# Linear attention with a gated MLP: a rewrite with two tokens to a row, 64x64 attention tiles and a written-out order

## The chip, the cores and the metric

The kernel runs on one core of one Trainium2 chip. Its time is the device time of one execution in microseconds (us). The times are medians over several runs; the profile is that of one execution.

## The reference

Inputs are q, k and v of shape (batch 4, heads 8, tokens 768, 64), a decay `lam` for each head, and the weights of a gated MLP. All are float32, as is the output (4, 768, 512).

```
# attention, token blocks of 64; Dmask[i,j] = lam^(i-j) for i >= j, else 0
intra = (q_b @ k_b.T * Dmask) @ v_b
inter = (q_b * lam^(pos+1)) @ state
out_b = intra + inter
state = lam^64 * state + (k_b * lam^(63-pos)).T @ v_b
# x = out as (4, 768, 512); then
h = relu(x @ w_in)                     # 512 -> 1024, split into u and v
v_n = (v - mean(v)) / sqrt(var(v) + 1e-6)
v_s = w_spatial @ v_n + b_spatial      # over the tokens, 768 x 768
out = (u * v_s) @ w_out                # 512 -> 512
```

The block size of the attention is free as far as the result goes: the sum over all earlier tokens with weight lam^(distance) is what is computed.

## The kernel before, in words

The work is cut into 12 steps: 4 batches, each with three steps of 256 tokens. A step is two chunks of 128 tokens.

- `load_step` (L65) issues five loads on SyncE's queue: k and v one chunk at a time (a partition holds one token of each chunk, so a row in memory is 64 floats, 256 bytes), and q with two neighbouring tokens to a partition (512 bytes). Buffers hold four steps.
- `cast_step` (L144) makes bf16: `kd`, k times a decay that is the same for every chunk (VectorE in the first three steps, GpSimd after), `qc` on ScalarE and `vc` on GpSimd.
- `trans_step` (L157) transposes `kd` and `qc` on TensorE (16 transposes, L163). ScalarE takes out `kT`; VectorE takes out `qT` times a table of decays `lq`.
- `scores_step` (L177): 16 matmuls (L189), heads in pairs on the two row halves of the array, 128 keys against 128 queries. VectorE multiplies by `amask` (L192), a causal mask with a factor for each head.
- `kv_step` (L198): the products of `kd` and `vc` (L207). The state of a chunk is the old one times lam^128 plus this product: `sd` (L218) and `s` (L219), on VectorE.
- `out_step` (L222): state times q (L242) and masked scores times v (L249) add up in PSUM; ScalarE takes `xT` out (L252).
- The MLP: `pv` (L269: 512 columns, ReLU, statistics, normalisation `vn`), `pu` (L292: the u half), `wt_piece` (L329: w_spatial transposed once), `pvs` (L301: six matmuls of 384 columns, then a seventh at L309 that adds the bias by a matrix of 1/128 against a broadcast bias; VectorE multiplies by u, L311), `po` (L316: the last product; a store of 256 rows for each step).

PSUM is four buffers of two banks, used in turn by all of these. TensorE and GpSimd run in the order of the program text: a step's scores, outputs and key-value products, with pieces of MLP work between them taken from a list (`fill`, `after_out`). On the other engines a scheduler places the instructions. All loads of q, k and v and all stores go through SyncE's queue; the weights go through GpSimd's queue, which casts them to bf16 on the way.

Of the kernel before, what the change touches and what calls it, by code (L numbers as in the profile page):

```python
# [8 lines left out]
FP32 = mybir.dt.float32  # L10
# [4 lines left out]
PE = mybir.EngineType.PE  # L15
# [3 lines left out]
def kernel(  # L19
# [13 lines left out]
    P = 128  # L33
# [4 lines left out]
    NBLK = S // P  # L38
    NG = H // 2
    NCH = DM // P  # L40
    NR = S // (2 * P)
    NS = B * NR
    T2 = 2 * P
    HW_ = S // 2

    const = ctx.enter_context(tc.tile_pool(name="const", bufs=1))
    wpool = ctx.enter_context(tc.tile_pool(name="wpool", bufs=1))
    fin = ctx.enter_context(tc.tile_pool(name="fin", bufs=4))
    att = ctx.enter_context(tc.tile_pool(name="att", bufs=3))
    gml = ctx.enter_context(tc.tile_pool(name="gml", bufs=1))  # L50
    xpool = ctx.enter_context(tc.tile_pool(name="xpool", bufs=2))
    small = ctx.enter_context(tc.tile_pool(name="small", bufs=2))
    ostg = ctx.enter_context(tc.tile_pool(name="ostg", bufs=3))
    psum = ctx.enter_context(tc.tile_pool(name="psum", bufs=4, space=bass.MemoryType.PSUM))

    def two_banks(shape, name, dt=FP32):
        return psum.tile(shape, dt, tag="ps", name=name)


    lam_bc = const.tile([P, H], FP32)  # L60
    nc.scalar.dma_start(out=lam_bc, in_=lam.unsqueeze(0).to_broadcast((P, H)))

    st = {}

    def load_step(n):  # L65
        b, r = divmod(n, NR)
        toks = slice(r * T2, (r + 1) * T2)
        q_in = fin.tile([P, H, 2, D], FP32, tag="q_in", name=f"q_in_{n}")
        k_in = fin.tile([P, H, 2, D], FP32, tag="k_in", name=f"k_in_{n}")
        v_in = fin.tile([P, H, 2, D], FP32, tag="v_in", name=f"v_in_{n}")  # L70
        for c in range(2):
            nc.sync.dma_start(out=k_in[:, :, c, :],  # L72
                              in_=k[b, :, toks][:, c * P:(c + 1) * P].rearrange("h p d -> p h d"))
        nc.sync.dma_start(out=q_in.rearrange("p h m d -> p h (m d)"),  # L74
                          in_=q[b, :, toks].rearrange("h (p m) d -> p h (m d)", m=2))
        for c in range(2):
            nc.sync.dma_start(out=v_in[:, :, c, :],  # L77
                              in_=v[b, :, toks][:, c * P:(c + 1) * P].rearrange("h p d -> p h d"))
        st[n] = {"q_in": q_in, "k_in": k_in, "v_in": v_in}

    load_step(0)
    ident = const.tile([P, P], BF16)
    make_identity(nc, ident)

    def iota_f(shape, pattern, base, mult, name):
        ti = const.tile(shape, I32, name=name + "_i")
        nc.gpsimd.iota(ti, pattern=pattern, base=base, channel_multiplier=mult)
        tf = const.tile(shape, FP32, name=name)
        nc.vector.tensor_copy(out=tf, in_=ti)
        return tf  # L90

    krev = iota_f([P, 1], [[0, 1]], P - 1, -1, "krev")

    qpos = iota_f([P, 2, 2, D], [[1, 2], [0, 2], [2, D]], 1, 0, "qpos")

    rel = iota_f([P, 2, D], [[1, 2], [2, D]], 0, -1, "rel")

    win_sb = wpool.tile([P, NCH, DFF], BF16)
    wout_sb = wpool.tile([P, NCH, DM], BF16)
    bsp_bc = wpool.tile([P, S], BF16)  # L100
    wt_sb = wpool.tile([P, NBLK, S], BF16)
    wsp_raw = wpool.tile([P, NBLK, S], BF16)

    def load_win(f0, f1):
        nc.gpsimd.dma_start(out=win_sb[:, :, f0:f1],
                            in_=moe_w_in.rearrange("(g p) f -> p g f", p=P)[:, :, f0:f1])

    load_win(DH, DFF)
    for n in range(1, 4):
        load_step(n)  # L110


    loglam = const.tile([P, H], FP32)
    nc.scalar.activation(out=loglam, in_=lam_bc, func=AF.Ln)
    logl = const.tile([P, NG], FP32)
    for hh in range(2):
        rows = slice(hh * D, (hh + 1) * D)
        nc.vector.tensor_copy(out=logl[rows, :], in_=loglam[rows, hh::2])
    ldec = const.tile([P, H], FP32)
    nc.scalar.activation(out=ldec, in_=loglam, func=AF.Exp, scale=krev[:, 0:1])  # L120
    lq = const.tile([P, NG, T2], BF16)
    for g in range(NG):
        nc.scalar.activation(out=lq[:, g, :], in_=qpos.rearrange("p m a d -> p (m a d)"),
                             func=AF.Exp, scale=logl[:, g:g + 1])
    l128 = const.tile([P, NG], FP32)
    nc.scalar.activation(out=l128, in_=logl, func=AF.Exp, scale=float(P))
    lm128 = const.tile([P, H], FP32)
    nc.scalar.activation(out=lm128, in_=loglam, func=AF.Exp, scale=-float(P))
    causal = const.tile([P, P], FP32)
    nc.vector.tensor_scalar(out=causal, in0=rel.rearrange("p m d -> p (m d)"), scalar1=0.0,  # L130
                            scalar2=None, op0=ALU.is_ge)
    amask = const.tile([P, 2, 2, 2, P], FP32)
    for h in range(H):
        nc.vector.tensor_scalar(out=amask[:, h // 4, h % 2, (h // 2) % 2, :], in0=causal,
                                scalar1=lm128[:, h:h + 1], scalar2=None, op0=ALU.mult)
    eps_t = const.tile([P, 1], FP32)
    nc.vector.memset(eps_t, 1e-6)
    oo128 = const.tile([P, P], BF16)
    nc.vector.memset(oo128, 1.0 / P)


    xT = {}

    def cast_step(n):  # L144
        s = st[n]
        kd = att.tile([P, 2, H, D], BF16, tag="kd", name=f"kd_{n}")
        qc = att.tile([P, 2, H, D], BF16, tag="qc", name=f"qc_{n}")
        vc = att.tile([P, H, 2, D], BF16, tag="vc", name=f"vc_{n}")
        eng = nc.vector if n < NR else nc.gpsimd
        eng.tensor_tensor(out=kd.rearrange("p c h d -> p h c d"), in0=s["k_in"],  # L150
                          in1=ldec.unsqueeze(2).unsqueeze(3).broadcast_to((P, H, 2, D)),
                          op=ALU.mult)
        nc.scalar.activation(out=qc.rearrange("p m h d -> p h m d"), in_=s["q_in"], func=AF.Copy)  # L153
        nc.gpsimd.tensor_copy(out=vc, in_=s["v_in"])  # L154
        s["kd"], s["qc"], s["vc"] = kd, qc, vc

    def trans_step(n):  # L157
        kd, qc = st[n]["kd"], st[n]["qc"]
        pt = two_banks([P, 2, NG, T2], f"pt_{n}", BF16)
        for j, src in ((0, kd), (1, qc)):  # L160
            for g in range(NG):
                for c in range(2):
                    nc.tensor.transpose(  # L163
                        out=pt[:, j, g, c * P:(c + 1) * P],
                        in_=src[:, c, 2 * g:2 * g + 2, :].rearrange("p h d -> p (h d)"),
                        identity=ident)
        kT = att.tile([P, NG, T2], BF16, tag="kT", name=f"kT_{n}")
        nc.scalar.activation(out=kT, in_=pt[:, 0], func=AF.Copy)  # L168
        qT = att.tile([P, NG, 2, 2, D], BF16, tag="qT", name=f"qT_{n}")
        nc.vector.tensor_tensor(out=qT.rearrange("p g m a d -> p g (m a d)"), in0=pt[:, 1],  # L170
                                in1=lq, op=ALU.mult)
        st[n]["qT"], st[n]["kT"] = qT, kT

    def qblk(n, g, hh, c):
        return st[n]["qT"][hh * D:(hh + 1) * D, g, :, c, :]

    def scores_step(n):  # L177


        kT = st[n]["kT"]  # L180
        a_sb = att.tile([P, 2, 2, 2, 2, P], BF16, tag="a_sb", bufs=2, name=f"a_{n}")
        st[n]["a"] = a_sb
        for i in range(2):
            pam = two_banks([P, 2, 2, 2, P], f"pam_{n}_{i}")
            for g2 in range(2):
                for c in range(2):
                    for hh in range(2):
                        g = 2 * i + g2
                        nc.tensor.matmul(out=pam[:, hh, g2, c, :],  # L189
                                         lhsT=kT[hh * D:(hh + 1) * D, g, c * P:(c + 1) * P],  # L190
                                         rhs=qblk(n, g, hh, c), start=True, stop=True)
            nc.vector.tensor_tensor(  # L192
                out=a_sb[:, i].rearrange("p h g c x -> p (h g) c x"),
                in0=pam.rearrange("p h g c x -> p (h g) c x"),
                in1=amask[:, i].rearrange("p h g x -> p (h g) x").unsqueeze(2)
                .broadcast_to((P, 4, 2, P)), op=ALU.mult)

    def kv_step(n):  # L198

        r = n % NR  # L200
        nb = 2 if r < NR - 1 else 1
# [20 lines left out]
    def out_step(n):  # L222
        b, r = divmod(n, NR)
        a_sb, vc = st[n]["a"], st[n]["vc"]
        if r == 0:
            xT[b] = xpool.tile([P, NR, NCH, T2], BF16, tag="xT", name=f"xT_{b}")
# [191 lines left out]
```

## Time and profile before

| | |
|---|---|
| median of 8 runs | 185.81 us (184.42 to 189.2) |
| profiled execution, its own time | 184.73 us |
| its span, first to last instruction | 183.0 us |
| mean granted clock of TensorE | 0.991 |
| TensorE busy | 144.2 us, 1530 matmuls |
| VectorE / ScalarE / GpSimd busy | 101.6 / 88.6 / 34.7 us |
| read from memory, written | 24.78 MB, 6.29 MB |

How to read it: the busy time of an engine is the union of its instructions' times. The slices of the page cut the span in 40 equal parts of 4.6 us, with the busy share of each in tenths. TensorE's matmuls are pipelined, and their ends are modelled, so the distance between starts tells more of their pace than the mean duration does. The page's chain follows the work that ended last back to its causes. A line of a group gives the source line, engine, operation, output and inputs, count, busy time and mean of one in ns, then the idle time in front of it and what ended it.

### The profile page before, as it was taken

To read this page: it belongs to the slowest core of one execution; us is meant where nothing else is said; L and a number is where in the kernel's file an instruction comes from. 1 tells how busy PE (TensorE), PEld (TensorE's weight loads), DVE (VectorE), ACT (ScalarE), POOL (GpSimd) and SP (SyncE) were. 2 spreads that over 40 slices of the span, in tenths; PEclk is the share of its full clock that TensorE was granted. 3 is DMA by queue.
4 is the path that set the end of the run, shared out by engine and by line. 5 is a ranking of instruction groups with operands and counts; after the bars stand their busy time and mean duration, and the time that the engine had idled before them with its cause. 6 is when DMAs were issued, how large, how long until landed. Compare 5 with 4: busy or idle time off the path is not lost.

```text
span 183.0 us, 3628 instructions
## 1 busy us (share of the span) xinstructions
PE 144.2 (79%) x1530; PEld 95.8 (52%) x1540; DVE 101.6 (56%) x191; ACT 88.6 (48%) x98; POOL 34.7 (19%) x35
## 2 busy tenths in 40 slices
PE   0004768538798599999998999999799999999980
PEld 0003655325477466556676665576675646565430
DVE  0119995730788944706989645198965713564400
ACT  3235324624667952277966405667530247650051
POOL 4004060024434524412406006020000000000000
PEclk9999999987999999999999999999999999999999
DMA  5989999998999999999999800630000036000035
GB/s 110 210 199 247 224 243 189 199 215 216 250 209 245 241 224 228 253 180 273 360 232 208 194 0 0 233 115 4 0 4 0 2 115 233 0 0 4 0 142 202
DMA packets 68337, 28.36 MB, mean 155 GB/s; under 512 B 50528, under 2 KB 65248, under 8 KB 68320
## 3 DMA queue, kind: packets, MB, share of 16 engines
q1 hardware_dynamic: 65664, 25.17, 57.0%
q0 software_dynamic: 2512, 2.95, 9.8%
q8 instruction: 12, 0.20, 0.5%
q14 instruction: 5, 0.04, 0.1%
q10 hardware_dynamic: 144, 0.00, 0.0%
HBM read 24.78 MB, written 6.29 MB: 170 GB/s over the span
## 4 chain that ended last, share of the span: by engine, by line
PE 51%; SPq 16%; DVE 11%; DMA 10%; ACT 8%; issue 2%; ACTq 0%
PE pvs L307 17%; PE po L322 11%; DMA q_in<-in_q_dram 10%; PE pv L277 8%; SPq L72 8%; SPq L77 6%; PE pu L297 5%; PE pt L163 3%; DVE a L192 3%; PE pvs L309 3%; DVE st L282 3%; ACT wt_sb L336 2%; SPq L74 2%; ACT vh L280 2%; ACT qc L153 2%
## 5 line engine op out<-in xcount | busy, mean ns | idle before, releaser
L307 PE MATMUL pvs<-wt_sb,vn 128*128 128x384 bf16 x192 | 37.1, 326 | 2.1 <-ACT wt_sb L336 2.0
L192 DVE TENSOR_TENSOR a<-pam,amask 128x1024 bf16<-128x1024 f32 x24 | 28.5, 1210 | 6.0 <-PE pam L189 6.0
L154 POOL CAST vc<-v_in 128x1024 bf16<-128x1024 f32 x12 | 12.9, 1071 | 78.1 <-DMA v_in<-in_v_dram 41.2
L252 ACT ACTIVATE xT<-pat 128x1024 bf16<-128x1024 f32 x12 | 15.8, 1318 | 22.6 <-PE pat L249 22.6
L307 PEld LDWEIGHTS <-vn 128*128 128x128 bf16 x192 | 18.6, 98 | 14.7 <-issue 2.2
L297 PE MATMUL pu<-xT,win_sb 128*128 128x256 bf16 x192 | 24.4, 285 | 1.9 <-DVE a L192 1.9
L311 DVE TENSOR_TENSOR gT<-pvs,uT 128x768 bf16<-128x768 f32 x16 | 15.3, 957 | 17.8 <-PE pvs L309 17.7
L277 PE MATMUL pv<-win_sb,xT 128*128 128x512 bf16 x90 | 23.8, 399 | 1.6 <-ACT xT L252 1.2
L322 PE MATMUL po<-wout_sb,gT 128*128 128x512 bf16 x92 | 21.7, 379 | 1.7 <-DVE a L192 1.1
L297 PEld LDWEIGHTS <-win_sb 128*128 128x128 bf16 x192 | 19.1, 102 | 5.7 <-issue 1.8
L163 PE MATMUL pt<-ident,kd 128*128 128x128 bf16 x96 | 8.6, 242 | 16.4 <-DVE kd L150 15.7
L325 ACT ACTIVATE o<-po 128x1024 f32<-128x1024 f32 x12 | 12.3, 1023 | 19.0 <-PE po L322 19.0
L282 DVE BATCH_NORM_STATS2 st<-vh 128x6 f32<-128x512 bf16 x24 | 15.6, 682 | 10.4 <-ACT vh L280 10.3
L153 ACT ACTIVATE qc<-q_in 128x1024 bf16<-128x1024 f32 x12 | 12.6, 1054 | 17.3 <-DMA q_in<-in_q_dram 17.2
L170 DVE TENSOR_TENSOR qT<-pt,lq 128x1024 bf16<-128x1024 bf16 x12 | 8.2, 684 | 19.8 <-ACT kT L168 19.8
L150 POOL TENSOR_TENSOR kd<-k_in,ldec 128x1024 bf16<-128x1024 f32 x9 | 17.1, 1896 | 8.3 <-DMA k_in<-in_k_dram 5.7
L168 ACT ACTIVATE kT<-pt 128x1024 bf16<-128x1024 bf16 x12 | 12.2, 1019 | 10.7 <-PE pt L163 10.7
L163 PEld LDWEIGHTS <-kd 128*128 128x128 bf16 x96 | 7.0, 109 | 18.4 <-DVE kd L150 15.8
L280 ACT ACTIVATE vh<-pv 128x1024 bf16<-128x1024 f32 x12 | 12.3, 1023 | 8.3 <-PE pv L277 8.3
L277 PEld LDWEIGHTS <-xT 128*128 128x128 bf16 x96 | 9.6, 102 | 11.7 <-issue 1.6
L322 PEld LDWEIGHTS <-gT 128*128 128x128 bf16 x96 | 9.2, 97 | 11.9 <-issue 1.0
L299 ACT ACTIVATE uT<-pu 128x1024 bf16<-128x1024 f32 x12 | 12.2, 1017 | 5.6 <-PE pu L297 5.5
(52 smaller groups left out, 143.9 us busy)
## 6 DMA issues: line engine op xcount, KB each, us to landing
k_in<-in_k_dram SPq DMA_DIRECT2D x24, 256.0 KB, 5.4
q_in<-in_q_dram SPq DMA_DIRECT2D x12, 512.0 KB, 5.8
v_in<-in_v_dram SPq DMA_DIRECT2D x24, 256.0 KB, 5.8
out_dram<-o SPq DMA_DIRECT2D x12, 512.0 KB, 3.3
wsp_raw<-in_moe_w_spatial_dram POOLq DMA_DIRECT2D x1, 1152.0 KB, 11.7
win_sb<-in_moe_w_in_dram POOLq DMA_DIRECT2D x2, 512.0 KB, 7.8
wout_sb<-in_moe_w_out_dram POOLq DMA_DIRECT2D x1, 512.0 KB, 14.9
bsp_bc<-in_moe_b_spatial_dram POOLq DMA_DIRECT2D x1, 192.0 KB, 12.1
```

The lines of the kernel that those rows point to most:

```text
L150: eng.tensor_tensor(out=kd.rearrange("p c h d -> p h c d"), in0=s["k_in"], in1=ldec.unsqueeze(2).unsqueeze(3).broadcast_to((P, H, 2, D)), ...
L153: nc.scalar.activation(out=qc.rearrange("p m h d -> p h m d"), in_=s["q_in"], func=AF.Copy)
L163: nc.tensor.transpose(out=pt[:, j, g, c * P:(c + 1) * P], in_=src[:, c, 2 * g:2 * g + 2, :].rearrange("p h d -> p (h d)"), identity=ident)
L192: nc.vector.tensor_tensor(out=a_sb[:, i].rearrange("p h g c x -> p (h g) c x"), in0=pam.rearrange("p h g c x -> p (h g) c x"), in1=amask[: ...
L252: nc.scalar.activation(out=xT[b][:, r].rearrange("p g (c d m) -> p (g c) m d", c=2, m=2), in_=po.rearrange("p g c (m d) -> p (g c) m d", m ...
L277: nc.tensor.matmul(out=ps[:, j], lhsT=x[:, r, c, j * P:(j + 1) * P], rhs=win_sb[:, c, DH:DFF], start=(c == 0), stop=(c == NCH - 1))
L280: nc.scalar.activation(out=vh[:, pair, :], in_=ps, func=AF.Relu)
L282: nc.vector.bn_stats(out=m["st6"][:, t, :], in_=vh[:, t, :])
L297: nc.tensor.matmul(out=ps[:, f], lhsT=win_sb[:, c, f * P:(f + 1) * P], rhs=x[:, r, c, :], start=(c == 0), stop=(c == NCH - 1))
L307: nc.tensor.matmul(out=ps[:, i, 0:HW_], lhsT=m["vn"][:, s, f * P:(f + 1) * P], rhs=wt_sb[:, s, cols], start=(s == 0), stop=False)
L311: nc.vector.tensor_tensor(out=m["gT"][:, f, :].rearrange("p (i x) -> p i x", i=2), in0=ps[:, :, 0:HW_], in1=m["uT"][:, f, :].rearrange("p ...
L322: nc.tensor.matmul(out=ps[:, j], lhsT=gT[:, c, t * P:(t + 1) * P], rhs=wout_sb[:, c, :], start=(c == 0), stop=(c == NCH - 1))
```

## The change

Nearly every line is new; the parts are these.

- Rows: partition p of a step holds tokens 2p and 2p+1 for q, k and v alike, one load each (12 loads each of q, k and v, 512 bytes to a row). The output is stored in two halves of 64 partitions for each 128 tokens.
- Decays: k is multiplied by lam^(384-pos) and q by lam^(pos-384), with pos the place in the whole batch of 768. The tables are made once with a power operation on GpSimd. Scores then need a mask of ones and zeros only, and the state of a batch is a plain sum: the key-value products add up in PSUM bank 7 over a whole batch, and after each chunk of 128 tokens a copy is taken (`SS`).
- Attention matmuls use 64 rows and 64 columns of the array each: scores (SC), state and intra products (AV), key-value products (KV). Output banks are chosen so that the two row halves write different banks.
- The bias: no matmul; VectorE adds a broadcast bias while it takes the product out of PSUM (GB), and a second instruction on VectorE or GpSimd multiplies by u (GM).
- PSUM is one tile of eight banks; the MLP evictions are of one bank (512 columns) instead of two. Casts, evictions, normalisations and gating products are spread over VectorE, ScalarE and GpSimd, one by one.
- The order of all engines is a list of tokens: name, step and piece, PSUM bank, engine (T TensorE, D VectorE, A ScalarE, P GpSimd, S SyncE). `GT` is a one-element copy on GpSimd from a loaded tile, put before a weight load in its queue.

```diff
-    def kv_step(n):
...
-                sd = att.tile([P, NG, D], FP32, tag="sd", name=f"sd_{n}_{c}")
-                nc.vector.tensor_tensor(out=sd, in0=prev, in1=lb, op=ALU.mult)
-                nc.vector.tensor_tensor(out=s_sb[:, c], in0=sd, in1=pkv[:, c], op=ALU.add)
...
-            nc.tensor.matmul(out=ps[:, i, 0:HW_], lhsT=oo128, rhs=bsp_bc[:, cols],
-                             start=False, stop=True)
...
+ORDER = """
+lam.A msk.P BS.S LQ.2.2.S LQ.0.2.S idn.P LK.0.2.S tab.P LQ.1.2.S BC.A LK.1.2.S LV.0.2.S QD.0.2.D TQ.0.6.T
+LV.1.2.S KD.0.2.P EQ.0.6.A LK.2.2.S QD.1.2.P TK.0.6.T EK.0.6.D LK.3.2.S SC.0.1.0.T KD.1.2.P TQ.1.6.T
...
+AV.1.1.2.T EK.2.6.D LV.3.2.S GT.0.3.P WI.1.P KV.1.1.T EX.1.0.2.A SC.2.1.0.T SC.2.0.4.T SS.1.1.A GT.0.3.P
+WS.0.P MK.2.1.0.D EX.1.1.3.A PV.0.1.6.T KD.3.2.P PV.1.1.3.T MK.2.0.4.D LQ.4.2.S VC.2.2.A PV.1.0.2.T EV.0.1.6.D
+GT.2.2.P WS.1.P EV.1.1.3.A TK.3.5.T BN.0.1.D EV.1.0.2.A PV.0.0.6.T BN.1.1.D AV.2.0.0.T BN.1.0.D EV.0.0.6.A
...
+PO.3.1.5.T GB.3.2.1.6.D PO.3.0.4.T GM.3.2.1.P EO.3.1.5.A PO.3.2.6.T ST.3.1.S EO.3.0.4.A PO.3.4.5.T ST.3.0.S
+EO.3.2.6.A PO.3.3.4.T ST.3.2.S PO.3.5.6.T EO.3.4.5.A ST.3.4.S EO.3.3.4.D ST.3.3.S EO.3.5.6.A ST.3.5.S
+"""
...
+    NIN, NCA, NTR, NA, NX, NO, NVS = 3, 2, 2, 2, 3, 3, 2
...
+    ps = psum.tile([P, 8, 512], FP32, name="ps")
+    SB = 7
...
+    def load(src, dst, n, h0, h1, e):
+        b, t = toks(n)
+        eng = {"S": nc.sync, "A": nc.scalar}[e]
+        eng.dma_start(out=dst[n % NIN][:, h0:h1].rearrange("p h m d -> p h (m d)"),
+                      in_=src[b, h0:h1, t].rearrange("h (p m) d -> p h (m d)", m=2))
...
+        for pos, ld in ((posk, ldk), (posq, ldq)):
+            nc.gpsimd.tensor_tensor(
+                out=ld, in0=lam_bc.unsqueeze(1).unsqueeze(3).broadcast_to((P, NR, H, 2)),
+                in1=pos.unsqueeze(2).broadcast_to((P, NR, H, 2)), op=ALU.pow)
...
+    def after(e, x, n):
+        nc.gpsimd.tensor_copy(out=seen, in_=(k_in, q_in, v_in)[x][n % NIN][0:1, 0, 0, 0:1])
...
+    def s_c(e, n, i, b):
+        pa = bank(b, 2).rearrange("p o (w j x) -> p o w j x", w=2, j=2)
+        for w in range(2):
+            u = 2 * i + w
+            for j in range(2):
+                for o in range(2):
+                    for c in range(2):
+                        nc.tensor.matmul(out=pa[row(c), o, w, j], lhsT=kT[n % NTR][row(o), u, j, c * Q64:(c + 1) * Q64],
+                                         rhs=qv(n, o, u, c), start=True, stop=True)
...
+    def k_v(e, n, c):
+        pkv = bank(SB)[:, 0:4 * D].rearrange("p (u d) -> p u d", u=4)
+        new = n % NR == 0 and c == 0
+        for u in range(4):
+            for m in range(2):
+                for o in range(2):
+                    nc.tensor.matmul(out=pkv[row(o), u], lhsT=kd[n % NCA][row(c), m, u, o, :],
+                                     rhs=vc[n % NCA][row(c), 4 * o + u, m, :],
+                                     start=new and u == 0 and m == 0, stop=(u == 3 and m == 1),
+                                     skip_group_check=True)
+
+    def s_s(e, n, c):
+        copy(e, s_sb[(2 * n + c) % 4].rearrange("p u d -> p (u d)"), bank(SB)[:, 0:4 * D])
...
+            for i in range(2):
+                for j in range(2):
+                    for c in range(2):
+                        for w in range(2):
+                            u = 2 * i + w
+                            nc.tensor.matmul(out=po[row(w), c ^ o, c, i], lhsT=vc[n % NCA][row(c), 4 * o + u, j, :],
+                                             rhs=a[row(c), i, o, w, j, :],
+                                             start=(r == 0 and o == 0 and i == 0 and j == 0),
+                                             stop=(i == 1 and j == 1), skip_group_check=True)
...
+    def w_t(e, s, b):
+        pw = bank(b, 2).bitcast(BF16).rearrange("p z x -> p (z x)")
+        for a in range(NT):
+            for m in range(2):
+                nc.tensor.transpose(out=pw[row(m), a * P:(a + 1) * P], in_=wsp_raw[:, a, s * P + m:(s + 1) * P:2],
+                                    identity=ident)
...
+    def g_b(e, bb, f, i, b):
+        HW = S // 2
+        nc.vector.tensor_tensor(out=vsb[(bb * 4 + f) % NVS][:, i * HW:(i + 1) * HW], in0=bank(b)[:, 0:HW],
+                                in1=bsp[:, i * HW:(i + 1) * HW], op=ALU.add)
...
+    with tc.manual_schedule():
+        for token in ORDER.split():
+            name, *args, e = token.split(".")
+            ops[name](e, *map(int, args))
```

The tokens that the text names: LQ, LK, LV loads; KD, QD decays of k and q; VC cast of v; TK, TQ transposes and EK, EQ their evictions; SC scores and MK the mask; KV key-value products; AV outputs and EX their eviction to `xT`; PV, PU the two halves of w_in and EV, EU their ReLU evictions; BN, RA, RD, VN statistics and normalisation; WI, WS, WO weight loads; WT, EW the transposed w_spatial; PW the spatial product; PO, EO, ST the last product, its eviction and its store.

## The prediction

> **What bounds the kernel now.** I read the page's busy shares and slices first, then busy time by stage, then the chain that ended last in order of time, then the timeline of one attention step.
>
> ```profile
> PE 144.2 (79%) x1530; PEld 95.8 (52%) x1540; DVE 101.6 (56%) x191; ACT 88.6 (48%) x98; POOL 34.7 (19%) x35
> ...
> PE   0004768538798599999998999999799999999980
> ...
> DMA  5989999998999999999999800630000036000035
> ```
>
> TensorE is the fullest engine, but not evenly: its first nine slices (41 us) hold gaps while DMA stands at 9 from the second slice on; from slice 12 TensorE is the full one. The stages say the same (after the span: busy us of PE, PEld, DVE, ACT, POOL, then clock, DMA share, GB/s):
>
> ```profile
> 0.00:15.00 15.00, 0.48 (x5) 0.49 (x6) 2.81 (x9) 5.92 (x11) 3.29 (x11) 1.00 0.86 175
> 15.00:30.00 15.00, 10.16 (x135) 8.75 (x134) 13.38 (x25) 5.70 (x6) 4.17 (x6) 1.00 1.20 232
> 30.00:45.00 15.00, 9.20 (x93) 5.40 (x92) 5.62 (x11) 5.96 (x7) 2.94 (x2) 0.89 1.08 211
> ...
> 75.00:90.00 15.00, 14.53 (x172) 9.28 (x171) 8.69 (x16) 10.95 (x12) 5.78 (x4) 1.00 1.09 273
> ```
>
> The chain names what ends last: a q transfer early, TensorE later, and a tail (start, duration, what):
>
> ```profile
> 29.94 13.57 DMA q_in<-in_q_dram
> ...
> 69.41 0.97 PE pvs L307 x6
> 70.38 0.16 PE pvs L309
> ...
> 80.64 1.73 PE po L322 x8
> ...
> 86.03 1.85 PE pu L297 x16
> ...
> 89.61 0.89 PE pt L163 x16
> ...
> 173.04 4.72 PE po L322 x21
> 177.84 1.02 ACT o L325
> ```
>
> Modelled ends overlap, so I price matmuls by starts. One attention step:
>
> ```profile
> 84.03 0.62 PE L189 MATMUL pam<-qT,kT 64*128 64x128 bf16 x16
> ...
> 84.58 0.64 PE L242 MATMUL pat<-qT,s 64*64 64x128 bf16 x16
> ...
> 85.14 0.64 PE L249 MATMUL pat<-a,vc 128*64 128x128 bf16 x16
> ...
> 85.62 0.42 PE L207 MATMUL pkv<-vc,kd 128*64 128x64 bf16 x16
> ...
> 85.97 1.92 PE L297 MATMUL pu<-xT,win_sb 128*128 128x256 bf16 x16
> ```
>
> From start to start: scores 0.55 us, state part 0.56, intra part 0.48, key-value products 0.35 for 16 each: 34, 35, 30 and 22 ns a matmul.
>
> TensorE's work before: pvs 32x0.97=31.0, bias 32x0.16=5.1, pu 12x1.85=22.2, pv and po 24x1.73=41.5, transposes 12x0.89=10.7, scores 12x0.55=6.6, state 10x0.56=5.6, intra 12x0.48=5.8, key-value 10x0.35=3.5, spatial transposes 36x0.056=2.0: 134.0 us. When it becomes dense at 45.16 us, 11.6 us of that is done (four steps of transposes, three of scores, two of outputs, 2.5 of key-values, one pv, one pu). The other 122.4 take the 132.6 us to 177.8: 92.3% dense. Then 5.2 us of tail. So 183.0 = 45.2 + 122.4/0.923 + 5.2.
>
> **The change part by part.**
>
> *TensorE's work.* The 32 bias matmuls go: -5.1. Scores and intra products double in number (192 to 384 each) at 64x64 with 128 columns; the state part keeps 160; key-value products go from 160 to 320 with 64 columns. No row has four 64x64 tiles side by side. Bounds for the 928 matmuls with 128 columns: 17 ns (half of the scores' 34, four tiles for two) to 35 ns (L242, the same shape with two tiles in turn, no gain). The pkv row shows LDWEIGHTS and matmul pairs issued every 22 ns, so 17 is doubtful; I take 25, near that row: 928x0.025=23.2. Key-value: 320x0.022=7.0 by pkv (35 at worst: 11.2; no gain expected, as one row half serves each group and two tiles alternate). Spatial transposes become 72 of half width: between 28 and 56 ns, 42 taken, 3.0. Sum: 134.0 - 5.1 - 21.5 (the old small ones) - 2.0 + 23.2 + 7.0 + 3.0 = 138.6. The new order changes between full and 64-wide work 60 times, where the old one went into and out of one such block a step (24). The scores' 0.55 us for eight pairs of 56 ns (0.45) leave at most 0.10 for a change: 36x0.10=3.6 at most, nothing at least, 1.0 taken. **Work after: 139.6 us, bounds 131 to 156.**
>
> The Trainium skill, TensorE: Matmul & The Clock Gate, section "Wait — 56ns, not 53.3ns?", holds that starts of matmuls never come closer than about 25 ns; the 22 ns of pkv here are a little under it. By it the lower bound would be 25 and the key-value products 8.0 us, 1.0 more. TensorEngine Tiling (Array Packing), section "Key Properties", speaks against the change: going to another tiling mode drains the array; it gives no price, and by it the 60 changes would lie nearer 3.6 than 1.0.
>
> *DMA and the start.* k and v move from two loads of 256-byte rows to one of 512-byte rows: 60 load issues on SP become 36, with 36864 packets for 61440. Stores go from 12 to 48 issues, behind loads in the same queue. Before, k of step 3 landed at 41.98 us, and by then 11.1 MB had been read (three steps of 1.57, 0.52, all weights 5.9): 0.28 MB/us. I take 0.30, bounds 0.28 (packet size makes no odds) and 0.36 (the page's best slice, 360 GB/s). Queue order is bias, q2, q0, k0, q1, k1, v0, v1, k2, k3, v2. Q0 lands near 7.5 us, k0 near 9. POOL then does k0, q1, k1, q2 at 1.9 us each (L150's row; each now two halves) and only behind them issues the first half of w_in at 17; landing took 6.6 to 9.0 us before, so about 25.6. TensorE's queue holds PV.0.1 there, with AV.2, KV.2 and all PU behind it. w_spatial follows behind gates on k3 and v2. Until its second half is in, 11.7 MB must come (bias 0.39, three steps 4.72, four more loads 2.1, w_in 2.1, w_spatial 2.36): 2+11.7/0.30=41 us. WT stands in front of everything of step 3. By then the batch's transposes 3.6, scores 2.4, outputs 3.4, key-values 1.8, pv 5.2 and pu 5.6 can be done: 22.0 us, of which 13.4 come after 25.6. POOL's table of powers is unseen in the trace: it lies before k0's landing; nothing to 5 us fits there, beyond that it delays TQ.0.
>
> *Vector engines.* Rows that these lean on, and one of sd's instructions (min/median/max ns):
>
> ```profile
> L192 DVE TENSOR_TENSOR a<-pam,amask 128x1024 bf16<-128x1024 f32 x24 | 28.5, 1210 | 6.0 <-PE pam L189 6.0
> ...
> L150 POOL TENSOR_TENSOR kd<-k_in,ldec 128x1024 bf16<-128x1024 f32 x9 | 17.1, 1896 | 8.3 <-DMA k_in<-in_k_dram 5.7
> ```
> ```profile
> L218 DVE TENSOR_TENSOR sd<-s,l x16: 404/425/2045, 21.9 to 134.4; 128x256 f32<-128x256 bf16 x16
> ```
>
> DVE loses the state recurrence (16x0.57+16x0.41+4x0.40=17.3) and the gating (15.3). It gains 32 bias adds of 384 (between L219's 0.41 for 256 and L311's 0.96 for 768: 0.55, 17.6), 12 gating products (6.6), 26 evictions of 512 (L215's 0.40 for 256: 0.66, 17.2), 11 copies of 1024 bf16 (L170's 0.68: 7.5) and 5 state copies; masks (28.5), statistics (20.4) and the rest stay: 111 us. ACT: 13 copies of 1.02, 70 of half size near 0.6, small ones: 78. POOL: 22 decays at 2.0, 16 normalisations (0.4 on DVE; 0.4 to 1.0 here), 20 gating products of 0.75, 6 casts of 1.04, weights: 83. All lie beside 139.6 of TensorE, so I cost them nothing on the path. Without that cover DVE is next. POOL's busier hours can hold DVE: sd's 404 ns became 2045 once. At risk are some 24 DVE instructions with SBUF inputs alone; each held 0.8 would cost 19, still covered.
>
> *Steady part and tail.* The order is written out with every engine's place; I leave density at 92.3%, though evictions of single banks give it more freedom and fewer spare buffers (two for three of cast and transposed tiles) less. Tail: a last eviction of 512, 0.6, and stores that landed in 3.3: 3.9 for 5.2.
>
> **Sum.** 41 + (139.6-22.0)/0.923 + 3.9 = 172.3 span. The profiled execution took 184.73 for 183.0 (1.7 outside): 174.0. It ran 1.1 under the median of 185.81: **175 us.**
>
> **The rivals.** *Small tiles bring nothing* (slower). All 1248 small matmuls cost L242's 35 ns: 43.7 for 30.2, and changes of mode 3.6 for 1.0: 16.1/0.923=17.4, so 192.5. It turns the sign when they average over 32 ns (10 us of work more). For it: L242 has this very shape and no better pace; against: its neighbours use only two tiles. Chance 0.25.
>
> *WT stalls TensorE* (no change). If packets bring nothing and POOL's queue issues w_spatial 5 us later, WT begins near 50: 184. For it: q's wait of 13.57 us before; against: weights now wait for the first loads instead of sharing with them. Chance 0.10.
>
> *Better packing.* 17 ns a tile and no price for changes: work 131; 21 done by 39, density 97% because the fixed order leaves no holes: 39+110/0.97+3.9+2.8=159. For it: evictions of 1.02 us halve, so banks come free sooner; against: the 22 ns row. Chance 0.18.
>
> Forecast 0.47. **How the numbers follow:** about 1% can be told from no change here. Faster by over 1%: forecast, better packing, a little of WT: 0.68; within 1%: 0.07; slower: 0.25. The range reaches from the better packing to small tiles at no gain: 160 to 191.
>
> **What would show it.** Right: pv dense from about 26 us, spatial transposes near 41, scores at 20 to 28 ns from start to start, about 139 us of TensorE work, DVE near 111 busy, last matmul near 168. Wrong: small matmuls at 33 ns or more; TensorE idle before WT beyond 45; TensorE waiting on POOL's decays or normalisations in the middle, which would break the 92.3%.

## The result, and the profile after

The changed kernel takes 196.48 us (median of 11 runs, 195.99 to 199.07); the kernel before took 186.78 us in 32 runs (183.91 to 189.97). The ratio, which here and in the experiments is of undisturbed runs alone while the times are medians of all, is 1.0624, 95% interval 1.0584 to 1.0663: the change makes the kernel 6% slower. The forecast was 175 us, range 160 to 191. The profiled execution has a span of 194.3 us at a mean granted clock of 0.979. Every span, where nothing else is said, is that of the one profiled execution, and the five executions of e2, for one, lie 2.6 us apart; the ratios are the firmer figures.

From the page of the kernel after, the busy times, three rows of the 40 slices (4.86 us each) and the shares of the chain:

```profile
PE 140.4 (72%) x2070; PEld 91.2 (47%) x2088; DVE 114.1 (59%) x190; ACT 71.3 (37%) x121; POOL 127.0 (65%) x109
...
PE   0000027969797876993999899987969999989960
...
POOL 3499996493695955299486878994197137393800
...
DMA  1999239999809599953999890000443110049186
...
PE 28%; POOL 27%; DVE 17%; DMA 13%; issue 9%; ACT 3%; SPq 1%; DVEq 0%; POOLq 0%; ACTq 0%
```

TensorE is no busier than before (140.4 us against 144.2) but its first five slices are empty. GpSimd went from 34.7 to 127.0 us and stands at 9 from the third slice to the sixth, where TensorE is still empty or has just begun; 27% of the chain is its work. DMA, full from the second slice on in the kernel before, drops to 2 and 3 in slices 5 and 6. By stage (after the span: busy us of PE, PEld, DVE, ACT, POOL, then clock, DMA share, GB/s):

```profile
0.00:15.00 15.00, 0.00 (x0) 0.00 (x0) 1.09 (x4) 2.17 (x2) 9.41 (x12) 1.00 0.73 204
15.00:30.00 15.00, 2.04 (x16) 1.61 (x16) 3.12 (x3) 1.02 (x1) 15.00 (x8) 1.00 0.60 152
30.00:45.00 15.00, 11.74 (x285) 9.19 (x287) 10.70 (x12) 5.91 (x10) 10.32 (x15) 1.00 1.07 247
75.00:90.00 15.00, 10.82 (x173) 6.79 (x171) 9.88 (x15) 7.79 (x13) 9.06 (x8) 1.00 0.73 177
```

From 15 to 30 us GpSimd is busy all the time and TensorE for 2.04 us, where before it had 10.16. From 75 to 90, where TensorE had 14.53 before, it has 10.82. So there are two losses: a late start, and holes in the middle of TensorE's work. The granted clock is 1.00 in all four stages.

The start, in the timeline (start, duration, engine, line, what, and in brackets the idle time before it and what ended it):

```profile
7.50 8.05 POOL L193 TENSOR_TENSOR ldk<-lam_bc,posk 128x48 f32<-128x48 f32 x1 [3.98 <-DMA lam_bc<-in_lam_dram]
15.53 8.00 POOL L193 TENSOR_TENSOR ldq<-lam_bc,posq 128x48 f32<-128x48 f32 x1
...
23.57 2.97 DVE L249 TENSOR_TENSOR qd<-q_in,ldq 128x512 bf16<-128x512 f32 x2 [20.68 <-POOL ldq L193]
...
26.60 1.03 PE L269 MATMUL ps<-ident,qd 128*128 128x128 bf16 x8 [26.60 <-DVE qd L249]
...
34.57 0.18 POOL L210 COPY seen<-k_in 1x1 f32<-1x1 f32 x1 [2.13 <-DMA k_in<-in_k_dram]
34.70 1.37 POOL L214 DMA_DIRECT2D win_sb<-in_moe_w_in_dram  x1
```

The two tables of powers, 48 numbers in a partition, take 8.0 us each. VectorE's first decay of q waits 20.68 us for the second, TensorE's first transpose 26.60 us. The copy at 34.57 is the `GT` in front of w_in; it ends a wait for a load of k. The weights land at 43.8, and there the first PV, the first product with w_in, starts. Loads wait too, since they need buffers that GpSimd's decays set free (SyncE's queue: what it waited for, us in total, times, the longest):

```profile
SPq L180 <- POOL kd L249: 31.1, 4, 16.0
```

One of the holes in the middle, first GpSimd's normalisations in the timeline, then the chain (start, duration, what), then how long TensorE's transposes waited for GpSimd's decays of q in the whole execution (us in total, times, the longest):

```profile
82.46 4.13 POOL L401 TENSOR_SCALAR vn<-vh,mv,rstd 128x512 bf16<-128x512 bf16 x2 [3.71 <-DVE rstd L397]
```
```profile
83.34 1.19 POOL vn L401
84.53 2.06 POOL vn L401
86.59 0.41 POOL qd L249
...
87.57 3.04 POOL qd L249 x3
90.66 0.97 PE ps L269 x8
```
```profile
PE ps L269 <- POOL qd L249: 4.3, 2, 3.4
```

GpSimd stands idle 3.71 us until the deviations (`rstd`) are there, then makes two normalisations, and the decays of q come behind them in its order. TensorE's transposes at 90.66 wait for these decays.

### The profile page after: what moved, and what is told of

The parts are those of the page before. It is cut to its first block, busy times and chain, and to the rows that moved or that the text cites. A ratio compares the mean times of both kernels' runs of the same rounds, so it can differ in the third digit from the quotient of the medians.

```text
span 194.3 us, 4902 instructions
## 1 busy us (share of the span) xinstructions
PE 140.4 (72%) x2070; PEld 91.2 (47%) x2088; DVE 114.1 (59%) x190; ACT 71.3 (37%) x121; POOL 127.0 (65%) x109
## 4 chain that ended last, share of the span: by engine, by line
PE 28%; POOL 27%; DVE 17%; DMA 13%; issue 9%; ACT 3%; SPq 1%; DVEq 0%; POOLq 0%; ACTq 0%
POOL vn L401 9%; PE ps L433 6%; PE ps L372 5%; PE ps L410 5%; PE ps L269 5%; DMA win_sb<-in_moe_w_in_dram 5%; POOL qd L249 4%; PE ps L449 4%; POOL ldq L193 4%; DMA q_in<-in_q_dram 4%; DMA lam_bc<-in_lam_dram 3%; POOL kd L249 3%; POOL ldk L193 3%; DVE gT L444 3%; DVE vsb L438 2%
## 5 line engine op out<-in xcount | busy, mean ns | idle before, releaser
L401 POOL TENSOR_SCALAR vn<-vh,mv,rstd 128x512 bf16<-128x512 bf16 x16 | 34.1, 2135 | 19.8 <-DVE rstd L397 19.7
L433 PE MATMUL ps<-wt_sb,vn 128*128 128x384 bf16 x192 | 35.0, 327 | 3.2 <-DVE vsb L438 2.3
L269 PE MATMUL ps<-ident,qd 128*128 128x128 bf16 x96 | 9.0, 249 | 32.5 <-DVE qd L249 26.6
L304 DVE TENSOR_TENSOR a_sb<-ps,m 128x1024 bf16<-128x1024 f32 x24 | 28.5, 1213 | 6.4 <-PE ps L300 4.0
L444 POOL TENSOR_TENSOR gT<-vsb,uT 128x384 bf16<-128x384 f32 x20 | 18.6, 935 | 19.0 <-DVE vsb L438 16.6
L249 POOL TENSOR_TENSOR kd<-k_in,ldk 128x512 bf16<-128x512 f32 x22 | 23.2, 1072 | 9.6 <-PE ps L316 9.6
L410 PE MATMUL ps<-xT,win_sb 128*128 128x256 bf16 x192 | 25.5, 279 | 0.1
L438 DVE TENSOR_TENSOR vsb<-ps,bsp 128x384 f32<-128x384 f32 x32 | 17.5, 550 | 12.5 <-PE ps L433 9.6
L372 PE MATMUL ps<-win_sb,xT 128*128 128x512 bf16 x83 | 22.5, 380 | 1.8 <-DMA win_sb<-in_moe_w_in_dram 0.8
L249 POOL TENSOR_TENSOR qd<-q_in,ldq 128x512 bf16<-128x512 f32 x22 | 22.9, 1062 | 0.6 <-DMA q_in<-in_q_dram 0.6
L269 PEld LDWEIGHTS <-qd 128*128 128x128 bf16 x96 | 7.1, 111 | 34.2 <-DVE qd L249 26.6
L449 PE MATMUL ps<-wout_sb,gT 128*128 128x512 bf16 x91 | 22.3, 384 | 0.4 <-issue 0.2
L164 ACT ACTIVATE qT<-ps 128x1024 bf16<-128x1024 bf16 x6 | 6.1, 1020 | 26.6 <-PE ps L269 26.6
```

What stands on the lines that cost most here:

```text
L164: nc.scalar.activation(out=o, in_=i, func=AF.Copy)
L249: vec(e).tensor_tensor(out=dst[n % NCA][:, :, :, pos, :].rearrange("p m u d -> p u m d"), in0=src[n % NIN][:, hs], in1=tab[:, r, hs].unsqu ...
L269: nc.tensor.transpose(out=pt[:, u, m], in_=src[n % NCA][:, m, u].rearrange("p o d -> p (o d)"), identity=ident)
L304: nc.vector.tensor_tensor(out=a_sb[n % NA][:, i].rearrange("p o w j x -> p (o w) (j x)"), in0=bank(b, 2).rearrange("p o (w y) -> p (o w) y ...
L372: nc.tensor.matmul(out=bank(b), lhsT=x[:, c, g], rhs=win_sb[:, g, DH:DFF], start=(g == 0), stop=(g == NCH - 1))
L401: vec(e).tensor_scalar(out=vn[p2][:, t], in0=vh[p2][:, t], scalar1=mv[p2][:, t, 0:1], scalar2=rstd[p2][:, t:t + 1], op0=ALU.subtract, op1= ...
```

## Experiments

Theory H says that the table of powers delays the start; theory N that the normalisations on GpSimd make the holes. The rival P takes up the prediction's slower case: the small tiles cost, and their pace is set by which tile the next matmul goes to.

**e1: the table by logarithm and exponential.** ScalarE and VectorE make the tables, q's first; GpSimd's power instruction is gone.

```diff
+        nc.scalar.activation(out=loglam, in_=lam_bc, func=AF.Ln)
...
-            nc.gpsimd.tensor_tensor(
-                out=ld, in0=lam_bc.unsqueeze(1)...,
-                in1=pos.unsqueeze(2)..., op=ALU.pow)
+            nc.vector.tensor_tensor(
+                out=ld, in0=loglam.unsqueeze(1)...,
+                in1=pos.unsqueeze(2)..., op=ALU.mult)
+            nc.scalar.activation(out=ld, in_=ld, func=AF.Exp)
```

> The decay tables come from Ln and Exp on ScalarE with a small product on VectorE, in place of two power operations of 8.0 us each at the head of GpSimd's queue. Theory H (head of the queue): the powers hold the first decay of q, so TensorE's first matmul falls from 26.6 us to about 13, and all weight loads behind it in GpSimd's queue move with it; span 194.3 -> about 181, ratio to before about 0.99. Theory N (normalisations on GpSimd pace the middle, whatever the start): the start moves, but the middle stays late; span 190 or more.

Measured: 189.44 us, 1.0211 of before (1.0132 to 1.0291); span 187.6, 6.7 less than after. In its timeline the tables are ready at 7.5 us and TensorE starts at 10.43, 16 us earlier. But w_in is issued only 8.6 us earlier:

```profile
26.02 0.18 POOL L213 COPY seen<-k_in 1x1 f32<-1x1 f32 x1 [7.02 <-DMA k_in<-in_k_dram]
26.15 0.99 POOL L217 DMA_DIRECT2D win_sb<-in_moe_w_in_dram  x1
```

GpSimd now stands idle 7.02 us in front of this `GT`, called the gate from here on. H holds for the start, but the span falls by half of what was expected (187.6 for 181), with another wait now in front of w_in.

**e2: all normalisations on VectorE.** The sixteen `VN.n.c.P` of the order become `VN.n.c.D`.

> All 24 normalisations on VectorE (0.42 to 0.53 us each) and none on GpSimd (2.07 us each); tables as in the changed kernel. Theory N: 33 us leave GpSimd, and the stretch from TensorE's first dense work at 43.9 us goes from 84% to about 92% dense, which is worth 10 to 13 us: span about 183. Theory H alone: the middle was covered, so VectorE's extra 7 us make it 194 to 198. Start of TensorE unchanged at 26.6 in both.

Measured: 191.31 us, 1.0312 (1.0226 to 1.0398); span 187.4, 6.9 less. GpSimd's busy time falls to 94.4 us and VectorE's rises to 120.2, only 6.1 more. N holds, again for less than expected (10 to 13 us). The first PV starts at 43.6, in after at 43.85, so nearly all of the gain comes from what follows it. This profiled execution was the shortest of the five; by the medians of the times the gain is 5.2 us.

**e3: both.**

> Both edits together. If H and N each hold a separate share, the gains add: span about 169 to 172, ratio to before 0.91 to 0.93. If both are one queue's backlog (what is taken off at one place is waited for at the other), the sum is smaller: 176 to 181.

Measured: 182.33 us, 0.9845 (0.9752 to 0.9939); span 180.5. The two gains add: the spans give 13.8 us together and 6.7 + 6.9 alone, the ratios 7.8 points together and 4.1 + 3.1 alone. The span is in the range that was expected of gains that do not add (176 to 181), only because each of them alone is smaller than expected. With both, the changed kernel is 1.5% faster than the one before.

**e4: scores in another order of tiles.** In after, four matmuls in a row go to four tiles (`o` and `c` choose rows and columns); in e4 two in a row go to the same tile. The work is the same.

```diff
-            for j in range(2):
-                for o in range(2):
-                    for c in range(2):
+            for o in range(2):
+                for c in range(2):
+                    for j in range(2):
```

> The changed kernel with the scores' loops in another order: the two matmuls of one tile (j) follow each other, where the changed kernel goes round all four tiles first. Theory P (rotation over four tiles is what gives 14 ns a matmul): pace of the 384 score matmuls goes from 14 to 25 ns or more, TensorE work +4 us, span +1 to +4. Rival (the issue of the pairs sets the pace): 14 ns and no change.

Measured: 196.69 us, 1.0595 (1.0498 to 1.0692), no different from after. One attention step in the timeline of after (durations are modelled, starts count):

```profile
96.78 0.31 PE L337 MATMUL ps<-qT,s_sb 64*64 64x128 bf16 x8
...
96.92 0.39 PE L346 MATMUL ps<-a_sb,vc 64*64 64x128 bf16 x16
...
97.19 0.42 PE L300 MATMUL ps<-qT,kT 64*64 64x128 bf16 x16
...
97.44 0.41 PE L316 MATMUL ps<-vc,kd 64*64 64x64 bf16 x16
...
97.68 0.41 PE L300 MATMUL ps<-qT,kT 64*64 64x128 bf16 x16
```

and in that of e4:

```profile
96.89 0.43 PE L300 MATMUL ps<-qT,kT 64*64 64x128 bf16 x16
...
97.14 0.42 PE L316 MATMUL ps<-vc,kd 64*64 64x64 bf16 x16
```

Sixteen scores (L300) take 0.25 us from start to start in both, 16 ns each. P falls: this order of tiles makes no difference. The prediction's slower rival (35 ns a matmul) falls by the pace in after itself, which is at the 17 ns of its better case.

**e5: no gates.** From here on the question is what stands between e3 and the forecast. Theory G: the gate. `GT.0.1` comes behind `LK.4` in the order, and with three buffers k of step 4 lies in the buffer of step 1, so the copy waits for the load of step 4. Theory B: too few buffers hold loads, decays and stores apart from that. e5 is e3 without its five `GT` tokens.

> The kernel with both edits (span 180.5), without the five one-element copies in front of the weight loads. The first of them copies from k's buffer 1, whose last writer in the order is the load of step 4, so w_in waits for k4 (27.4 us). Theory G: this gate is what puts the first pv at 35.9 us where 25.6 was forecast; without it w_in is issued near 19.6 and lands near 28, and the span falls by 5 to 8 us, to 173 to 176. Rival (total bytes set when dense work can start, the gate only chooses who comes first): first pv earlier, but k, q and v of steps 2 to 4 come later, span 179 to 183.

Measured: 177.17 us in four runs (172.90 to 177.60), too wide apart for a ratio. The trace (span 175.4) is read for the start alone: w_in is issued at 18.90, with the first PV at 28.8, for 27.52 and 35.91 in e3. G holds for the start.

**e6 and e7: more buffers, with and without gates.** e6 is e3 with four input buffers, three of `kd` and `vc` and six for the output; e7 is e6 without `GT`. In both the cast of v of step 4 reads v of step 8, which the order has loaded over it, so their output is not the reference's and they stand for times alone.

```diff
-    NIN, NCA, NTR, NA, NX, NO, NVS = 3, 2, 2, 2, 3, 3, 2
+    NIN, NCA, NTR, NA, NX, NO, NVS = 4, 3, 2, 2, 3, 6, 2
```

> The kernel with both edits, with four input buffers for three, three cast buffers for two and six output buffers for three; same order. Theory B: waits of the evictions for stores (17.0 us in all) and of GpSimd's decays for a free cast buffer (5.0 us near 71) reach TensorE; span 176 to 178. Rival: these waits lie beside TensorE's work; 179.5 to 181.5.

> Both edits, no gates and more buffers. If G and B both hold: 169 to 172. If only G: 173 to 176. If neither: 179 to 182.

Measured: e6 171.69 us, 0.916 (0.9082 to 0.9239); e7 173.93 us, 0.928 (0.9203 to 0.9357). They don't part G from B: with four buffers the copy of `GT.0.1` reads the buffer of step 1 before step 5 is loaded into it, and w_in goes out at 19.31 in e6 with the gates in place. What e7 shows is that, with buffers enough, taking the gates away gains nothing.

**e8: the normalisation with constants.** After, where GpSimd's sixteen normalisations subtract 0 and multiply by 1 instead of reading two columns; these tiles stay unnormalised. It asks whether the columns make the 2.07 us.

> The changed kernel; GpSimd's 16 normalisations use constants 0 and 1 in place of the two columns of mean and deviation, so that those tiles are left unnormalised. If the two per-partition columns are what costs 2.07 us on GpSimd, one falls to near 1.0 us (a cast of 1024 takes 1.03, a product of 384 0.94). If the kind of operation or the two steps cost it, it stays at 2.0.

Measured, in one run: 193.6 us, span 191.9. The tile `vn` in after, then in e8 (min/median/max ns, first and last start):

```profile
L401 POOL TENSOR_SCALAR vn<-vh,mv,rstd x16: 2062/2072/2521, 50.5 to 173.1; 128x512 bf16<-128x512 bf16 x16
L401 DVE TENSOR_SCALAR vn<-vh,mv,rstd x8: 405/451/849, 52.1 to 168.6; 128x512 bf16<-128x512 bf16 x8
```
```profile
L402 POOL TENSOR_SCALAR vn<-vh x16: 1912/1923/2231, 48.3 to 167.5; 128x512 bf16<-128x512 bf16 x16
```

The columns cost 0.15 us. The rest is the instruction itself (whether its kind or its two operations cost it was not tested), and VectorE does the same in 0.45. Without the columns GpSimd doesn't wait for the statistics either, yet the span is only 2.4 us shorter, in a single run.

**e9, e10, e11: buffers one kind at a time, on e3.** e9 has six output buffers, e10 five input buffers (then the copy of `GT.0.1` reads the buffer of steps 1 and 6, and nothing of step 4), e11 five input, three of `kd` and `vc`, and six output.

```diff
-    NIN, NCA, NTR, NA, NX, NO, NVS = 3, 2, 2, 2, 3, 3, 2
+    NIN, NCA, NTR, NA, NX, NO, NVS = 3, 2, 2, 2, 3, 6, 2   # e9
+    NIN, NCA, NTR, NA, NX, NO, NVS = 5, 2, 2, 2, 3, 3, 2   # e10
+    NIN, NCA, NTR, NA, NX, NO, NVS = 5, 3, 2, 2, 3, 6, 2   # e11, e12
```

> Both edits (span 180.5) and six output buffers for three, nothing else. The evictions waited 17 us for stores there, once 5.4 at a stretch. Theory O: some of it is on TensorE's path, since the queue of banks behind an eviction stands still: span 176 to 178. Rival: 180 to 181.

> Both edits and five input buffers for three, nothing else. With five, the first gate copies from k of step 1, not of step 4, so w_in is issued near 19. Theory G+I (the gate and the loads that wait for a free input buffer): 172 to 175, as the run without gates (175.4) or better. If input buffers themselves matter beyond the gate, it is below 173.

> Both edits, five input, three cast and six output buffers, the order unchanged. If the shares add: 168 to 171, ratio to before 0.90 to 0.925, faster than both kernels.

Measured: e9 180.03 us, 0.9745 (0.9631 to 0.9859), span 177.7; e10 175.98 us, 0.9432 (0.933 to 0.9535), span 171.8; e11 172.86 us, 0.9368 (0.9296 to 0.9441), span 170.4. Against e3's span of 180.5 that is 2.8 us for the output buffers, 8.7 for the input buffers and 10.1 for all. In the ratios it is 1.0, 4.1 and 4.8 points, so that the gain of the output buffers is not clear of the noise, and the shares add only roughly. e11 beats both kernels: 6.3% under the one before, where 7.5 to 10% was expected. The PE row of its page, and stages as shown of after:

```profile
PE   0027796977899969999976998999999999999940
```
```profile
15.00:30.00 15.00, 12.80 (x289) 9.87 (x286) 11.55 (x13) 5.91 (x10) 13.60 (x18) 1.00 1.21 259
...
75.00:90.00 15.00, 13.67 (x329) 10.02 (x332) 13.05 (x20) 9.48 (x16) 10.32 (x11) 1.00 1.03 276
```

and the issue of w_in in its timeline, without a wait in front:

```profile
18.86 0.18 POOL L213 COPY seen<-k_in 1x1 f32<-1x1 f32 x1
18.98 0.94 POOL L217 DMA_DIRECT2D win_sb<-in_moe_w_in_dram  x1
```

TensorE has 12.80 us from 15 to 30 and 13.67 from 75 to 90, with its total busy time the same as in after (139.9 for 140.4).

e10 was to be below 173 if input buffers matter beyond the gate, and its span is 171.8. That bound was set against e5's profiled 175.4, and e5 has a run of 172.90 us, span 171.2. The shortest and longest runs of the two are alike: 172.90 and 177.60 in e5, without gates and with three input buffers, 173.55 and 178.54 in e10 (taken in another set of runs). So nothing shows that input buffers bring more than the end of the gate's wait.

**e12: the buffers alone, on after.**

> The changed kernel (span 194.3; powers and 16 normalisations on GpSimd) with the same buffers as the last run. If buffers are a share of their own, the same 10 us come off: 184 to 186. If the loss there was GpSimd's, which buffers don't help: 190 to 194. If more buffers let GpSimd run ahead and so hide the powers and normalisations: below 182.

Measured: 193.45 us, 1.0434 (1.0304 to 1.0564), span 189.3. By spans the buffers bring 5.0 us here and 10.1 on e3, by the ratios 1.9 points and 4.8; the spans of its runs, 189.3 to 192.4, lie about the 190 to 194 that was expected if the loss is GpSimd's. As GpSimd computes powers until 23 us, its queue reaches the gate only at 31.86, without a wait there, and the first PV starts at 41.1. More buffers don't repair an engine that is late.

## Why the prediction was wrong

The spans close the account. After has 194.3; without the two costs on GpSimd 180.5 (13.8 less); with the buffers as well, 170.4 (10.1 less). The forecast's span was 172.3. What it took for granted was a kernel without these two losses. Its range ended at 191, below the 192.5 of the slower rival that it was said to reach; 196.48 lies beyond both.

1. **The table of powers.** The step read "nothing to 5 us fits there, beyond that it delays TQ.0". It measured 16.0 us. The bound came from the room before k0's landing, not from any price: the condition was named and the upper end was left where it hurt nothing. Even that room was not there: GpSimd waited for `lam` until 7.50, and k0 was expected near 9. The first transpose came at 26.6, for 10.43 in e1. That is the first failed step, worth 6.7 us of span (e1). The kernel before makes its decays by a logarithm and exponentials on ScalarE (`loglam` 0.21 us, L114; `ldec` 0.28, L120), so no row of it had a power.

2. **GpSimd's normalisations.** The step priced sixteen at "0.4 to 1.0 here", in a sum of 83 us for GpSimd which was to "lie beside 139.6 of TensorE, so I cost them nothing on the path". They take 2.07 us each, 34.1 in all, and GpSimd's sum is 127.0, 16.0 of it the powers. The average still leaves room beside TensorE's; the queue does not. A normalisation waits for VectorE's statistics (19.7 us in seven waits) and stands in one order with decays and gating products, so a late one makes what follows late, as the decays of q at 86.59 above. The prediction's last part named this ("TensorE waiting on POOL's decays or normalisations in the middle") and gave it neither a price nor a chance. Worth 6.9 us of span (e2), 5.2 by the medians; how much of it is the price and how much the wait for statistics was not parted. The Trainium skill, GPSIMD Engine Reference, section "4.1 Engine selection", calls an elementwise operation with one input on GpSimd roughly line-rate. The rows above don't agree: 2072 ns is 4.6 times VectorE's 451, and 1923 with constants still 4.3 times. GpSimd's cast of v, 1.03 us for 1024 elements against 0.68 on VectorE, is nearer to it.

3. **The gate.** The forecast let w_in go out at 17, behind GpSimd's decays, and w_spatial alone wait at gates. Once the powers were gone, the copy waited for k of step 4 until 26.02 in e1 and 27.39 in e3. With it out of the way w_in went out at 18.98 and PV began at 28.1 in e11, against 17 and 25.6 forecast: the step's durations were about right, its reading of the order was not. The prediction counted spare buffers for cast and transposed tiles alone ("two for three"). It left out that the input buffers go from four steps to three, and it is with three that k of step 4 lies in the buffer of step 1; in e6, with four, w_in went out at 19.31. e10 prices gate and input buffers together at 8.7 us; e5's shortest run says that the gate may be all of it.

4. **Density.** 92.3% was carried over from before. In after, from the first PV at 43.85 to the end of TensorE's work at 187.6, 143.7 us hold about 122.7 us of work, 85%. In e11 the same work lies between 28.1 and 163.7: 90%. So the number was nearly right for this order once the normalisations are on VectorE and the buffers suffice, and wrong for after.

5. **The matmuls.** Forecast 25 ns for the small ones, bounds 17 to 35. From the starts shown: scores 0.25 us for 16 and key-value products 0.24 (15 to 16 ns, where 22 and no gain was forecast), state part 0.14 for 8, intra part 0.27 for 16. The chain, which goes by ends, gives the state part 0.24, with what the change from full width costs, and the intra part 0.22. With these two TensorE's work sums to about 129.5 us (pvs 31.1, pu 22.2, pv and po 41.6, transposes 10.8, small ones 20.9, spatial transposes 2.9), under the lower bound of 131. The Trainium skill's floor of about 25 ns between starts, however small the matmul (TensorE: Matmul & The Clock Gate, section "Wait — 56ns, not 53.3ns?"), does not hold for these tiles here. The forecast of TensorE's work missed by 10 us in the good direction, and so the rival with a chance of 0.25, "small tiles bring nothing", was the wrong slower case. The nearest case was "WT stalls TensorE" (chance 0.10), with the transposes of w_spatial near 50 because GpSimd issues it 5 us late. They began at 58.1 in after and at 43.8 in e11, so one of the prediction's signs of being wrong, TensorE idle before WT beyond 45, was there. But that case gave 184, and none had GpSimd's own work late through the whole kernel.

6. **The tail.** Forecast 3.9 us after TensorE's end, measured 6.7 in after, and also 6.7 in e11. The prediction counted "a last eviction of 512, 0.6, and stores that landed in 3.3", but the stores are issued one by one, and the last twelve take 7.5 us to issue (e11's timeline, SyncE's queue):

```profile
160.10 7.52 SPq L461 DMA_DIRECT2D out_dram<-o_sb  x12
```

In e11 the last eviction ends at 164.34, but the issues, 0.63 us each without a gap, go on to 167.62; the end comes 2.8 us after that. That the same change made 48 stores of 12 was said in the prediction, and not carried to its tail. A version with fewer last stores, or with two queues for them, was not tried.

7. **What held.** The rate of the first loads: slices of 290 GB/s in the page of e11 against 0.30 MB/us, or 300 GB/s, assumed. VectorE 114.1 us for 111, ScalarE 71.3 for 78. The bias matmuls are gone, and VectorE adds the bias at 550 ns apiece for 0.55 us forecast. e11's span splits into 28.1 for the start, 122.7 at 90%, and 6.7. That its 170.4 lies near the forecast's 172.3 is partly luck: 10 us less of matmuls paid for a later start, a lower density and a longer tail.

What stays open: e1's start is 9.0 us earlier at the first PV and its span 6.7 shorter, and where the other 2.3 go was not traced.

## What to carry to other kernels

An operation that no row shows needs a price from both sides even when it seems covered: take the dearest reading, put it at the head of its engine's queue, and look at who stands behind it before calling it hidden. Where an order is written by hand, read each wait in the order of the tokens and with the buffer's number (step modulo buffers), since a one-element copy for step 1 can mean the load of step 4. And a rewrite that seems to fail can hold its gain: compare the busy time of the engine that should bound it, here 140 us in 194, and ask which queue keeps it waiting.

## What the runs showed of the hardware

- A power on GpSimd: 8.0 us for 48 float32 elements in each partition, 167 ns for each; the same table by a logarithm (0.21 us), a product on VectorE (0.21) and an exponential (0.24), with one load of a function table of 1.28 us between them in e1.
- A subtract and multiply on GpSimd, 512 bf16 elements: 2.07 us with columns, 1.92 with constants, 4 ns an element. Its decay of 512 float32 takes 1.04 us and its cast of 1024 1.03.
- VectorE's gating product, two inputs in SBUF, takes 558 ns in the median and took 3157 once beside GpSimd:

```profile
67.24 3.16 DVE L444 TENSOR_TENSOR gT<-vsb,uT 128x384 bf16<-128x384 f32 x1
```

  In e3, without GpSimd's normalisations, its longest was 815 ns. That GpSimd held it was not tested by itself.
- Matmuls on 64x64 tiles: 16 ns from start to start for scores of 128 columns, with four tiles in turn (after) or two in a row to the same one (e4); 15 ns for key-value products of 64 columns, which alternate between two tiles of one row half.
